# A two-layer decode kernel: VectorE's order inside a head, the place of TensorE's loops in the fetched code, and the order of the work between the layers

## The chip, the core and the metric

The kernel runs on one core of one Trainium2 chip. The metric is device time in microseconds (us) of one execution; less is better. All engines of the core (TensorE, VectorE, ScalarE, GpSimd and SyncE) run their own instruction streams and wait for one another on semaphores. SyncE here does nothing but start DMA transfers.

## What is computed

Two layers over one token for a batch of 2 (width D = 576), each layer an attention over a cache and a mixer MLP, with one set of weights and one cache used in both layers:

```python
def _A_ref(x, k_cache, v_cache, wq, wo):        # H, Dh = 32, 128; Sk = 16384
    q = (x @ wq).reshape(B, Sq, H, Dh).transpose(0, 2, 1, 3)
    scores = einsum("bhqd,bhkd->bhqk", q, k_cache) * (Dh ** -0.5)
    p = softmax(scores, axis=-1)
    o = einsum("bhqk,bhkd->bhqd", p, v_cache)
    return o.transpose(0, 2, 1, 3).reshape(B, Sq, H * Dh) @ wo

def _B_ref(x, w1, w2, w3, w4):
    h = gelu(layernorm(x) @ w1)
    ...                                          # quarters of h shifted along S, which is 1: all zero
    hs = concatenate([g0, g1, g2, g3]) @ w2
    x1 = x + hs
    return x1 + gelu(layernorm(x1) @ w3) @ w4

for layer in range(2):
    x = x + _A_ref(layernorm(x), k_cache, v_cache, wq, wo)
    x = x + _B_ref(layernorm(x), w1, w2, w3, w4)
```

The caches are 2 x 32 x 16384 x 128 in bf16, so each layer reads 268 MB of K and as much of V: 64 pairs of batch and head (called heads from here on), each with one K tile and one V tile of 4.19 MB. Of layer 0's tiles three of K and two of V stay for layer 1.

## The kernel before, in words

**Memory.** One SBUF buffer `mem` holds six places of 32 KB per partition (`slot`, L451) and a small area ahead of them for transposed K (`kt`). A K or V tile fills one place; the parts of the weights wo, w3, w4 and wq share two places between the layers (`plan_all`, L509). The list of transfers is fixed in that function, and `Store.pump` (L291) hands them to SyncE strictly in that order: a transfer is issued (L98) when its place has been released by its last reader, and everything behind it on SyncE waits with it.

**Waits.** Every operation is recorded in a `Graph` with the names that it reads and writes; `_add` (L49) finds what it depends on and `_waits` (L118) leaves out whatever is already covered by another wait of the same engine. An operation can be recorded with `to=`, which means that its semaphore is one that only that engine reads. If another engine has to wait for such an operation, `_stand_in` (L136) takes the next operation of the same engine that raises the general semaphore. When a tile has landed, GpSimd passes it on to TensorE and VectorE as a relay (`landed`, L1099; "POOLq L187" in the profile).

**One head.** Its 128 blocks of 128 keys are split. Half of K goes over TensorE in eight chunks of eight blocks: transposes (L1161), evacuation by ScalarE (L1177), scores with q as a column (L1187). The other half goes over VectorE in four pairs of a product (L1218) and a sum (L1222), with q broadcast over the partitions (`qb`). Then VectorE takes the maximum (L1228, L1230, L1232), GpSimd the maximum over partitions (L1235), ScalarE the exponentials (L1243, L1245, L1249), and TensorE multiplies p with V in four chunks (`pv`, L1275); VectorE keeps the sum (`keep_o`, L1256). The next head's q is prepared by `q_broadcast` (L1115): q as a column (L1112), the diagonal of q (L1118) on VectorE, a matmul with ones (L1122) on TensorE, a copy (L1125) on ScalarE.

**The loops.** `attention` (L1001) records 63 heads in turns of three and has TensorE, ScalarE and VectorE run them as a loop of 21 turns (`Fori`, L253). Three heads make one turn. In head s of the loop the K side of s runs beside the softmax and the V side of head s - 1. `head_slot` says at which instruction of a fetched block of code the loop's first instruction is to stand; it is 0 for all three. In VectorE's order within a head, `keep_o` and the maximum of head s - 1 come behind the second pair, and q of head s + 1 behind the fourth.

**Between the layers.** `last_head` (L1068) finishes layer 0's last head, normalises all heads (`shares`, `normed`), sorts them for the projection (`dealt`; its selection matrix `every` lies in the buffer of the products) and multiplies with wo in five steps (`heads_projection` over `rows_step`, L903). Each step frees its place for the next weights. `two_norms` (L746) computes both layer norms of the mixer at once, `spread_tail` (L794) spreads the last 64 columns of x, `cols_projection` (L830) does w3 and then wq, `between_norms` (L768) keeps the sum for later, `gelu` and `groups_projection` do w4, `input_norm` and `q_projection` give layer 1's q. Idle time of TensorE and ScalarE is used for layer 1's first head, whose K is held: `ahead` (L672) records transposes of it, `lay` (L689) writes them back transposed. When q is there, `early_scores` (L1194) needs only matmuls, 14 chunks of them; VectorE's share of these scores is copied to `s_dve` (L1041), and layer 1's loop begins.

The order of VectorE in a head is set by these lines of `attention`, where c counts the eight chunks and n is 4:

```python
if c % n in (0, 2):
    self.dots(l, s, u, c // n, c % n // 2)
if c == 2 * n - 2:
    self.q_broadcast(s + 1)
if c == LEAD:                       # 2
    self.keep_o(s - 2)
    self.softmax_max(s - 1)
```

Of the kernel before, what the change touches and what calls it, by code (L numbers as in the profile page):

```python
# [5 lines left out]
ALU = mybir.AluOpType  # L6
# [5 lines left out]
LN_EPS = 1e-5  # L12
# [20 lines left out]
class Graph:  # L33
# [111 lines left out]
    def emit(self):  # L145
        nc = self.nc
        self._waits()
        for o in self.all:
# [3 lines left out]
            if o.relay:  # L152
                o.needed = True
        for e, first, n, turns, _ in self.loops:
# [38 lines left out]
        def runner(e):  # L193
            ops = self.ops[e]
            loops = {first: x for en, first, *x in self.loops if en == e}

            def run(eng):
                seen, taken = {}, {}
                i = 0
                while i < len(ops):  # L200
                    if i in loops:
                        n, turns, step = loops[i]
                        self._loop(eng, e, i, n, turns, step, taken, seen, sems, wait, needs, emit_op)
# [13 lines left out]

    def _loop(self, eng, e, first, n, turns, step, taken, seen, sems, wait, needs, emit_op):

# [32 lines left out]
        me = eng.engine  # L252
        with self.nc.Fori(0, (turns - 1) * step + 1, step, engines=OrderedEngineSet([me]), head_slot={me: 0}) as turn:  # L253
            self.shift = turn
# [78 lines left out]
class KB:  # L333
# [13 lines left out]
    WO_CUT = 5  # L347
    PK = ["prod", "gT", "hf", "every"]
    GROUPS = (6, 6, 6, 6, 6, 3, 2, 1)

    def __init__(self, nc, A_x, K, V, wq, wo, w1, w2, w3, w4, out):
# [157 lines left out]
    def plan_all(self):  # L509
# [236 lines left out]
    def two_norms(self, l):  # L746
# [8 lines left out]
        self.tt(s[:, 5, :], self.mv[:, 0, :], hm[:, 0, :], ALU.mult, ["mv", "hm"], ["s5"])  # L755
        self.tt(s[:, 5, :], self.mv[:, 2, :], s[:, 5, :], ALU.subtract, ["mv", "s5"], ["s5"])
        self.stt(s[:, 5, :], s[:, 5, :], 2.0, s[:, 3, :], ALU.mult, ALU.mult, ["s5", "s3"], ["s5"])
        self.tt(s[:, 4, :], s[:, 4, :], s[:, 5, :], ALU.add, ["s4", "s5"], ["s4"])
        self.recip(s[:, 6, :], s[:, 4, :], ["s4"], ["s6"])
# [3 lines left out]
        self.centred(self.x, "x")  # L763
        self.tt(self.kb(self.y0), self.kb(self.xc), self.over_k(s[:, 3, :]), ALU.mult, ["prod", "s3"], ["prod"])
        self.tt(self.kb(self.y), self.kb(self.y0), self.hsc[:, :, :], ALU.add, ["prod", "hsc"], ["prod"])
        self.tt(self.xn[:, :, :], self.kb(self.y), self.over_k(s[:, 7, :]), ALU.mult, ["prod", "s7"], ["xn"])

    def between_norms(self):  # L768

        KT, TL = self.KT, self.TL  # L770
        n, y0 = KT - 1, self.kb(self.y0)
        self.tt(self.x1[:, 0:n, :], y0[:, 0:n, :], self.hs[:, 0:n, :], ALU.add, ["prod", "hs"], ["x1"])
        self.tt(self.x1[TL:, n, :], y0[TL:, n, :], self.hs[TL:, n, :], ALU.add, ["prod", "hs"], ["x1"])
        self.dv(lambda e: e.tensor_copy(out=self.xb[:, 0:n, :], in_=y0[:, 0:n, :]), reads=["prod"], writes=["xb"])
        self.dv(lambda e: e.tensor_copy(out=self.xb[TL:, n, :], in_=y0[TL:, n, :]), reads=["prod"], writes=["xb"])
        self.tt(self.x, self.x, self.x1[:, :, :], ALU.add, ["x", "x1"], ["x"])
# [195 lines left out]
    def groups_projection(self, l):  # L972
        n = len(self.GROUPS)
        for i, (a, b) in enumerate(self.cuts["w4", l]):
            nm = ("w4", l, i)
            self.rows_step(self.store.buf(nm), a, b, self.mps, lambda k: self.gT[:, k * self.B:(k + 1) * self.B],
                           "gT", "mps", nm, i == 0)
            if i < 5:
                self.ahead(l, 1)
            if i < 6:  # L980
                self.lay(l, 1)
# [19 lines left out]
    def attention(self, l):  # L1001
# [27 lines left out]
        else:  # L1029
            self.lay(0, len(self.laid))  # L1030
            assert self.made == len(self.early) and len(self.held_over) == LEAD
            pend += self.held_over
            for h, b, col in sorted(self.early):
                self.early_scores(l, o[0], h * self.BP + b, col)
                if (h, b) == (0, self.CH):
                    self.q_broadcast(1)
            self.store.claim("kt", 0, self.AUX)
            for x in pend:
                self.evacuate(x[3])
            w = self.NB - 2 * self.PB  # L1040
            self.dv(lambda e: e.tensor_copy(out=self.s_dve[0][:, 0:w], in_=self.sps[2][:, 2 * self.PB:self.NB]),  # L1041
                    reads=[("sps", 2)], writes=[("s_dve", 0)], to="vector")
# [25 lines left out]
    def last_head(self, l, s, u):  # L1068
# [4 lines left out]
        i, hg = self.ident[:, :], self.HG  # L1073
        every = bass.AP(tensor=i.tensor, offset=i.offset, ap=[list(i.ap[0]), [1, hg], [0, hg], [hg, 128 // hg]])
        self.dv(lambda e: e.tensor_copy(out=self.every.rearrange("p (j h m) -> p j h m", j=hg, h=hg), in_=every),
                reads=["ident"], writes=["prod", "every"])
        self.softmax_max(s)
        self.keep_o(s - 1)
# [7 lines left out]
        self.landed("v", u, False)  # L1086
        self.pv(l, s, u, 0)
        self.heads_projection(l, 0)
        for g in range(1, 4):
            self.pv(l, s, u, g)  # L1090
        self.keep_o(s, None)
        self.normed(l, first, U)
        self.heads_projection(l, 1)
        self.dealt(late, U, self.sps[0], ("sps", 0), self.masked[1], self.oB[:, :], "oB")
        for i in range(2, len(self.cuts["wo", l])):
# [19 lines left out]
    def q_broadcast(self, s):  # L1115
        i = s % self.NS
        self.q_column(s)
        self.dv(lambda e: e.tensor_scalar(out=self.diag[:, :], in0=self.ident[:, :], scalar1=self.g.column(self.q_f, s),  # L1118
                                          scalar2=None, op0=ALU.mult), reads=["ident", "q_f"], writes=["diag"],
                to="tensor")  # L1120
        qps = self.sps[i][:, 256:384]
        self.pe(lambda pe: pe.matmul(qps, lhsT=self.ones_bf[:, :], rhs=self.diag[:, :],  # L1122
# [71 lines left out]
    def early_scores(self, l, u, b0, col):  # L1194

        to = 0 if col < 2 * self.PB else 2
        ps = self.sps[to]

        nm, buf, keys = self.tile("k", u, b0, self.CH)

        def f(pe):
# [3 lines left out]
            return ins  # L1205
        self.pe(f, reads=[("q_col", 0)] + keys, writes=[("sps", to)])
        self.used(l, "k", u, b0, self.CH)
# [157 lines left out]
```

## Time and profile before

| what | value |
|---|---|
| runs | 2554.43, 2555.88 and 2558.73 us, median 2555.88 |
| the profiled execution | 2555.16 us |
| its span, from the first to the last instruction | 2553.4 us |
| mean granted clock of TensorE | 0.572 |
| busy TensorE, VectorE, ScalarE, GpSimd | 64%, 74%, 48%, 6% of the span |
| moved by DMA | 1094.82 MB in 44761 packets, 429 GB/s over the span |

The profile is one execution as the hardware recorded it. Rows of the timeline give the start in us from the first instruction, the duration (of a group of operations of one kind, up to the last), the engine, the line in the kernel, the operation, what is written and read and in what shape, and how many; a bracket at the end is the idle time of that engine ahead of it and what ended it, where "issue" means that nothing in the profile explains the idle time. Engine names are PE for TensorE, DVE for VectorE, ACT for ScalarE, POOL for GpSimd, SPq for SyncE's queue of DMA starts; "PEld" is the loading of a matmul's weights. Rows of the DMA view give the number of transfers, the size of one and the us from issue to landing. Rows of the table by stage give the stage, its length, the busy time of PE, PEld, DVE, ACT and POOL with the number of instructions in brackets, the granted clock, the share of time in which the DMA engines were busy (it can come out above 1), and GB/s.

### The profile page before, as it was taken

The numbers are of one execution on the slowest core, as the hardware profiler recorded it, in microseconds if no ns is written. First come the engines' busy times: TensorE is split into PE (matmuls) and PEld (weight loads), VectorE is DVE, ScalarE is ACT, GpSimd is POOL, SyncE is SP. The second block draws the span as 40 slices with busy tenths as digits, with TensorE's granted clock in tenths as the row PEclk, the third lists the DMA queues.
The fourth block names the chain that finished last, engine by engine and source line by source line (L and its number), as shares of the span: only waits on it lengthen the run. The fifth ranks groups of instructions, "written<-read, shape, count | busy, mean of one in ns | idle before, by whom it ended". The sixth has DMA issues, their size and how long they took to land.

```text
span 2553.4 us, 75093 instructions
## 1 busy us (share of the span) xinstructions
PE 1629.1 (64%) x34456; PEld 1592.5 (62%) x34456; DVE 1889.3 (74%) x1924; ACT 1215.6 (48%) x1831; POOL 160.5 (6%) x151
## 2 busy tenths in 40 slices
PE   3766666656666665666687756666665666666566
PEld 3766566656656665666677756656665666666565
DVE  4877777777777777777649877777777777777774
ACT  2544444544444454444456544444454444445442
POOL 0000000000000000000000000000000000000000
PEclk8555655555555555555555565555555555555555
DMA  9999999999999999999999999999999999999999
GB/s 410 429 433 431 432 432 431 432 431 433 431 432 432 432 433 430 434 430 432 424 398 428 431 432 432 431 432 431 433 431 433 431 431 433 432 432 431 432 432 383
DMA packets 44761, 1094.82 MB, mean 429 GB/s; under 512 B 4906, under 2 KB 6318, under 8 KB 9390
## 3 DMA queue, kind: packets, MB, share of 16 engines
q1 hardware_dynamic: 44718, 1094.23, 99.9%
q8 instruction: 29, 0.48, 0.1%
q14 instruction: 14, 0.11, 0.0%
HBM read 1094.21 MB, written 0.00 MB: 429 GB/s over the span
## 4 chain that ended last, share of the span: by engine, by line
DMA 63%; DVE 21%; issue 9%; PE 5%; DVEq 0%; SPq 0%; ACT 0%; POOLq 0%; ACTq 0%
DMA mem<-in_A_k_cache_dram 61%; DVE prod L1218 10%; DVE s_dve L1222 9%; DMA mem<-in_B_w_dram 2%; PE tps L1161 2%; PE mps L1275 2%; PE sps L1122 1%; DMA mem<-in_A_wq_dram 0%; PE sps L1187 0%; DVE diag L1118 0%; PE sps L903 0%; DVE mx L1232 0%; DVE q_col L1112 0%; DVE o_acc L1256 0%; DVE mx L1230 0%
## 5 line engine op out<-in xcount | busy, mean ns | idle before, releaser
L1177 ACT ACTIVATE mem<-tps 128x1024 bf16<-128x1024 bf16 x1018 | 1030.1, 1024 | 848.5 <-PE tps L1161 826.8
L1222 DVE TENSOR_REDUCE s_dve<-prod 128x16 f32<-128x2048 bf16 x508 | 1161.2, 2286 | 17.4
L1161 PE MATMUL tps<-ident,mem 128*128 128x128 bf16 x8256 | 1011.0, 301 | 152.9 <-POOLq L187 148.1
L1218 DVE TENSOR_TENSOR prod<-mem,qb 128x2048 bf16<-128x2048 bf16 x508 | 621.3, 1223 | 534.0 <-POOLq L187 512.2
L1275 PE MATMUL mps<-p,mem 128*128 128x1 bf16 x16384 | 515.5, 166 | 605.7 <-ACT p L1249 605.7
L1275 PEld LDWEIGHTS mps<-p,mem 128*128 128x128 bf16 x16384 | 487.8, 105 | 616.5 <-ACT p L1249 616.4
L1161 PEld LDWEIGHTS tps<-ident,mem 128*128 128x128 bf16 x8256 | 770.0, 136 | 162.5 <-POOLq L187 157.4
L1187 PEld LDWEIGHTS sps<-q_col,mem 128*128 128x128 bf16 x8144 | 410.5, 113 | 5.0 <-ACT mem L1177 4.8
L1187 PE MATMUL sps<-q_col,mem 128*128 128x1 bf16 x8144 | 398.2, 170 | 4.3 <-ACT mem L1177 4.1
L1235 POOL PARTITION_ALL_REDUCE mx<-mx x128 | 158.6, 1239 | 2339.4 <-DVE mx L1232 2339.4
L1243 ACT ACTIVATE mx<-mx 128x1 f32<-128x1 f32 x128 | 25.9, 203 | 338.8 <-POOL mx L1235 338.8
L1122 PE MATMUL sps<-diag,ones_bf 128*128 128x128 bf16 x129 | 37.0, 287 | 114.0 <-DVE diag L1118 113.9
L1122 PEld LDWEIGHTS sps<-diag,ones_bf 128*128 128x128 bf16 x129 | 13.4, 104 | 124.6 <-DVE diag L1118 124.6
L1125 ACT ACTIVATE qb<-sps 128x128 bf16<-128x128 f32 x129 | 35.8, 278 | 61.7 <-PE sps L1122 61.7
L1245 ACT ACTIVATE p<-s_dve,mx 128x64 bf16<-128x64 f32 x128 | 44.5, 348 | 15.4
L1249 ACT ACTIVATE p<-sps,mx 128x64 bf16<-128x64 f32 x128 | 37.6, 293 | 0.0
L1230 DVE TENSOR_REDUCE mx<-sps 128x1 f32<-128x64 f32 x128 | 27.3, 213 | 6.2 <-PE sps L1187 6.2
L1118 DVE TENSOR_SCALAR diag<-ident,q_f 128x128 bf16<-128x128 bf16 x129 | 31.6, 245 | 0.0
L1228 DVE TENSOR_REDUCE mx<-s_dve 128x1 f32<-128x64 f32 x128 | 26.6, 208 | 0.0
L830 PE MATMUL sps<-xn,mem 128*128 128x2 bf16 x544 | 21.5, 174 | 6.7 <-DMA mem<-in_A_wq_dram 4.8
L1256 DVE COPY o_acc<-mps 128x1 f32 (+1 forms) x130 | 19.2, 148 | 8.4 <-PE mps L1275 8.4
L830 PEld LDWEIGHTS sps<-xn,mem 128*128 128x128 bf16 x544 | 20.6, 122 | 7.8 <-DMA mem<-in_A_wq_dram 5.5
(113 smaller groups left out, 229.1 us busy)
## 6 DMA issues: line engine op xcount, KB each, us to landing
mem<-in_A_v_cache_dram SPq DMA_DIRECT2D x125, 4096.0 KB, 47.2
mem<-in_A_k_cache_dram SPq DMA_DIRECT2D x124, 4096.0 KB, 40.9
mem<-in_B_w_dram SPq DMA_DIRECT2D x10, 864.0 KB, 15.3
mem<-in_A_wq_dram SPq DMA_DIRECT2D x8, 1024.0 KB, 12.6
mem<-in_B_w_dram SPq DMA_DIRECT2D x7, 1152.0 KB, 15.4
mem<-in_A_wo_dram SPq DMA_DIRECT2D x6, 1152.0 KB, 35.8
mem<-in_A_v_cache_dram SPq DMA_DIRECT2D x4, 1024.0 KB, 8.8
mem<-in_A_k_cache_dram SPq DMA_DIRECT2D x2, 2048.0 KB, 10.2
```

Source lines behind the costliest of these rows:

```text
L830: ins = pe.matmul(out[:, m * B:(m + 1) * B], lhsT=buf[:, c:c + 127 * d + 1:d], rhs=self.xn[:, k, :], start=first and m == lo, stop=False, ...
L1122: self.pe(lambda pe: pe.matmul(qps, lhsT=self.ones_bf[:, :], rhs=self.diag[:, :], start=True, stop=True, skip_group_check=True), reads=["o ...
L1125: self.act(lambda e: e.activation(out=self.qb[s % self.NS][:, :], in_=qps, func=ACT.Copy), reads=[("qps", i)], writes=[("qb", s % self.NS) ...
L1161: ins = pe.transpose(self.tps[t][:, j * 128:(j + 1) * 128], buf[:, j * 128:(j + 1) * 128], self.ident[:, :])
L1177: self.act(lambda e: e.activation(out=self.kt[k], in_=self.tps[t][:, :].rearrange("p (i c) -> p i c", i=self.CH), func=ACT.Copy), reads=[( ...
L1187: ins = pe.matmul(self.sps[sp][:, c * self.CH + j:c * self.CH + j + 1], lhsT=self.kt[k][:, j, :], rhs=self.q_col[:, sp:sp + 1], start=True ...
L1218: self.dv(lambda e: e.tensor_tensor(out=prod, in0=buf.rearrange("p (j d) -> p j d", d=128), in1=qbc, op=ALU.mult), reads=[("qb", s % self. ...
L1222: self.dv(lambda e: e.tensor_reduce(out=sd[:, c0:c0 + DB], in_=prod, axis=AX.X, op=ALU.add), reads=["prod"], writes=[("s_dve", s % self.NS ...
L1235: self.pool(lambda e: e.partition_all_reduce(self.mx[:, 3, m:m + 1], self.mx[:, 2, m:m + 1], channels=128, reduce_op=ROP.max), reads=[("mx ...
L1245: self.act(lambda e: e.activation(out=p[:, n:self.NB], in_=self.s_dve[s % self.NS][:, :], func=ACT.Exp, bias=self.mx[:, 4, m:m + 1], scale ...
L1249: self.act(lambda e: e.activation(out=p[:, 0:n], in_=self.sps[i][:, 0:n], func=ACT.Exp, bias=self.mx[:, 4, m:m + 1], scale=self.scale, acc ...
L1275: ins = pe.matmul(self.mps[:, 448:449], lhsT=buf[:, j * 128:(j + 1) * 128], rhs=p[:, col:col + 1], start=(h == 0 and b == 0), stop=(h == 1 ...
```

## The change

Five edits (the numbers are only for reading):

1. **VectorE in a head.** In a head of the loop `keep_o`, the maximum and the next head's q column and diagonal come directly behind the first pair of products, ahead of the other three. The matmul and the copy that follow the diagonal are recorded ahead of the exponentials (c == 4), not at c == 6.
2. **The loops' places.** TensorE's loop starts at slot 200 of a fetched block in layer 0 and at slot 60 in layer 1; ScalarE's and VectorE's stay at 0.
3. **The last head.** The copy into `every` comes behind the maximum; all four p x V chunks and the sums come ahead of the first projection with wo; `ahead` and `lay` are dealt out anew.
4. **Norms and w3.** In `two_norms` the operations are reordered, and y0 and y get names of their own. The first rows of w3 come in two halves (w3 then has seven transfers instead of six).
5. **Early scores.** They run in the order in which the list has them (VectorE's share first), and VectorE's share goes to `mps` instead of `sps[2]`, so that its copy is recorded after eight of the 14 chunks.

```diff
-    def loop(self, first, turns, step):
+    def loop(self, first, turns, step, slot):
...
-            self.loops.append((e, a, n // turns, turns, step))
+            self.loops.append((e, a, n // turns, turns, step, slot if e == "tensor" else 0))
...
-        with self.nc.Fori(..., head_slot={me: 0}) as turn:
+        with self.nc.Fori(..., head_slot={me: slot}) as turn:
...
+    HEAD = (200, 60)
...
-        self.plan_cols("w3", 0, self.w3, [full(0, mt, a), full(1, mt, a + w3r), full(2, mt, a + 2 * w3r),
-                                          full(4, mt, a + 3 * w3r), (3, 0, mt // 2, 0), (3, mt // 2, mt, a)])
+        self.plan_cols("w3", 0, self.w3, [(0, 0, mt // 2, a), (0, mt // 2, mt, a + w3r // 2),
+                                          full(1, mt, a + w3r), full(2, mt, a + 2 * w3r), full(4, mt, a + 3 * w3r),
+                                          (3, 0, mt // 2, 0), (3, mt // 2, mt, a)])
...
         self.ahead(l, 3)
-        self.scale_of()
+        (s0, s5, s1, s5, s2, centred, s3, s4, s5, y0, s4, y, s6, s7: each operation as before, in this order)
...
-            for h, b, col in sorted(self.early):
+            w = self.NB - 2 * self.PB
+            for i, (h, b, col) in enumerate(self.early):
                 self.early_scores(l, o[0], h * self.BP + b, col)
-                if (h, b) == (0, self.CH):
+                if i == 1:
                     self.q_broadcast(1)
+                if i == w // self.CH - 1:
+                    self.dv(lambda e: e.tensor_copy(out=self.s_dve[0][:, 0:w], in_=self.mps[:, 2 * self.PB:self.NB]),
+                            reads=["mps"], writes=[("s_dve", 0)], to="vector")
...
-            self.dv(lambda e: e.tensor_copy(out=self.s_dve[0][:, 0:w], in_=self.sps[2][:, 2 * self.PB:self.NB]),
-                    reads=[("sps", 2)], writes=[("s_dve", 0)], to="vector")
...
                 step(s, c, True)
-                if c % n in (0, 2):
-                    self.dots(l, s, u, c // n, c % n // 2)
-                if c == 2 * n - 2:
-                    self.q_broadcast(s + 1)
                 if c == LEAD:
                     self.keep_o(s - 2)
                     self.softmax_max(s - 1)
+                    self.q_diag(s + 1)
+                if c % n in (0, 2):
+                    self.dots(l, s, u, c // n, c % n // 2)
                 if c == n:
+                    self.q_spread(s + 1)
                     self.softmax_exp(s - 1)
...
-        self.g.loop(first, (U - 1) // NS, NS)
+        self.g.loop(first, (U - 1) // NS, NS, self.HEAD[l])
...
-        self.dv(lambda e: e.tensor_copy(out=self.every..., in_=every), reads=["ident"], writes=["prod", "every"])
         self.softmax_max(s)
         self.keep_o(s - 1)
+        self.dv(lambda e: e.tensor_copy(out=self.every..., in_=every), reads=["ident"], writes=["prod", "every"])
...
+        self.ahead(l, 2)
         self.softmax_exp(s)
         self.touch(ACT.Sqrt)
-        self.lay(l, 1)
-        self.shares(first, U)
+        self.lay(l, 3)
         self.landed("v", u, False)
-        self.pv(l, s, u, 0)
-        self.heads_projection(l, 0)
-        for g in range(1, 4):
+        for g in range(4):
             self.pv(l, s, u, g)
+        self.shares(first, U)
         self.keep_o(s, None)
+        self.heads_projection(l, 0)
         self.normed(l, first, U)
-        self.heads_projection(l, 1)
         self.dealt(late, U, self.sps[0], ("sps", 0), self.masked[1], self.oB[:, :], "oB")
+        self.heads_projection(l, 1)
+        self.ahead(l, 1)
+        self.lay(l, 1)
...
     def q_broadcast(self, s):
-        (column, diagonal, matmul with ones, copy)
+        self.q_diag(s)      # column, diagonal
+        self.q_spread(s)    # matmul with ones, copy
```

More of the change, by code (lines that the diff above doesn't have):

```diff
@@ L153, in emit @@
                 o.needed = True
-        for e, first, n, turns, _ in self.loops:
+        for e, first, n, turns, *_ in self.loops:
             for i in range(n):
@@ L201, in run @@
                     if i in loops:
-                        n, turns, step = loops[i]
-                        self._loop(eng, e, i, n, turns, step, taken, seen, sems, wait, needs, emit_op)
+                        n, turns, step, slot = loops[i]
+                        self._loop(eng, e, i, n, turns, step, slot, taken, seen, sems, wait, needs, emit_op)
                         i += n * turns
@@ L216, in emit, with _loop @@
                     sect(runner(e))
-    def _loop(self, eng, e, first, n, turns, step, taken, seen, sems, wait, needs, emit_op):
+    def _loop(self, eng, e, first, n, turns, step, slot, taken, seen, sems, wait, needs, emit_op):
         ops = self.ops[e]
@@ L252, in _loop @@
         me = eng.engine
-        with self.nc.Fori(0, (turns - 1) * step + 1, step, engines=OrderedEngineSet([me]), head_slot={me: 0}) as turn:
+        with self.nc.Fori(0, (turns - 1) * step + 1, step, engines=OrderedEngineSet([me]), head_slot={me: slot}) as turn:
             self.shift = turn
@@ L347 @@
     WO_CUT = 5
-    PK = ["prod", "gT", "hf", "every"]
+    PK = ["prod", "gT", "hf", "every", "y0", "y"]
     GROUPS = (6, 6, 6, 6, 6, 3, 2, 1)
+    HEAD = (200, 60)
     def __init__(self, nc, A_x, K, V, wq, wo, w1, w2, w3, w4, out):
@@ L762, in two_norms @@
         self.lay(l, 4)
[L763 to L766, printed above, removed]
+        self.tt(self.xn[:, :, :], y, self.over_k(s[:, 7, :]), ALU.mult, ["y", "s7"], ["xn"])
     def between_norms(self):
@@ L1081, in last_head @@
         self.dealt(0, late, self.sps[2], ("sps", 2), self.masked[0], self.oA[:, :], "oA")
+        self.ahead(l, 2)
         self.softmax_exp(s)
         self.touch(ACT.Sqrt)
-        self.lay(l, 1)
-        self.shares(first, U)
-        self.landed("v", u, False)
-        self.pv(l, s, u, 0)
-        self.heads_projection(l, 0)
-        for g in range(1, 4):
-            self.pv(l, s, u, g)
-        self.keep_o(s, None)
-        self.normed(l, first, U)
-        self.heads_projection(l, 1)
-        self.dealt(late, U, self.sps[0], ("sps", 0), self.masked[1], self.oB[:, :], "oB")
+        self.lay(l, 3)
+        self.landed("v", u, False)
+        for g in range(4):
+            self.pv(l, s, u, g)
+        self.shares(first, U)
+        self.keep_o(s, None)
+        self.heads_projection(l, 0)
+        self.normed(l, first, U)
+        self.dealt(late, U, self.sps[0], ("sps", 0), self.masked[1], self.oB[:, :], "oB")
+        self.heads_projection(l, 1)
+        self.ahead(l, 1)
+        self.lay(l, 1)
         for i in range(2, len(self.cuts["wo", l])):
@@ L1194, in early_scores @@
     def early_scores(self, l, u, b0, col):
-        to = 0 if col < 2 * self.PB else 2
-        ps = self.sps[to]
+        ps, pk = (self.sps[0], ("sps", 0)) if col < 2 * self.PB else (self.mps, "mps")
         nm, buf, keys = self.tile("k", u, b0, self.CH)
@@ L1205, in f @@
             return ins
-        self.pe(f, reads=[("q_col", 0)] + keys, writes=[("sps", to)])
+        self.pe(f, reads=[("q_col", 0)] + keys, writes=[pk])
         self.used(l, "k", u, b0, self.CH)
```

32 lines of the change are left out of this document (20 added, 12 removed).

## The prediction

> **What bounds the kernel now.** I read the page's head, queues and transfers first, then the busy table by stage, then the timeline of one head.
>
> ```profile
> span 2553.4 us, 75093 instructions
> ...
> q8 instruction: 29, 0.48, 0.1%
> ...
> HBM read 1094.21 MB, written 0.00 MB: 429 GB/s over the span
> ...
> mem<-in_A_v_cache_dram SPq DMA_DIRECT2D x125, 4096.0 KB, 47.2
> mem<-in_A_k_cache_dram SPq DMA_DIRECT2D x124, 4096.0 KB, 40.9
> ```
>
> The kernel is a stream of 1094 MB, and a K needs 40.9 us to land: it stands in a queue. The table by stage says where the stream is not at its rate:
>
> ```profile
> 100.00:1260.00 1160.00, 731.76 (x15375) 716.93 (x15373) 877.48 (x841) 557.83 (x839) 75.19 (x60) 0.57 1.00 432
> 1260.00:1282.00 22.00, 17.72 (x431) 16.95 (x429) 6.97 (x36) 6.28 (x14) 0.35 (x1) 0.50 0.98 395
> 1282.00:1294.00 12.00, 9.78 (x217) 9.20 (x216) 0.98 (x6) 5.28 (x8) 0.00 (x0) 0.50 0.97 354
> 1294.00:1330.00 36.00, 27.66 (x592) 26.16 (x589) 14.85 (x34) 18.62 (x26) 1.25 (x1) 0.50 1.02 427
> 1330.00:1352.00 22.00, 18.36 (x405) 18.05 (x403) 20.31 (x20) 12.54 (x18) 1.25 (x1) 0.58 0.96 395
> 1352.00:2510.00 1158.00, 744.38 (x15677) 729.62 (x15675) 892.96 (x855) 568.06 (x855) 76.42 (x61) 0.57 1.00 431
> ```
>
> The last number of a row is GB/s. Both long stages run at 431 to 432. Only the seam between the layers loses: 22 x (1 - 395/432) = 1.9, 12 x (1 - 354/432) = 2.2, 36 x (1 - 427/432) = 0.4 and 22 x (1 - 395/432) = 1.9 us, together 6.4 us. That is all that this change could win there, and whatever it adds to those gaps it pays in full, because from 1352 on the stream never pauses again: the end shifts as the stream shifts. 0.2% of the run, 5.1 us, is about what a measurement of this kernel can tell from no change.
>
> **The change part by part.** First the heads in the long stages, where VectorE's order is new:
>
> ```profile
> 716.76 0.33 SPq L98 DMA_DIRECT2D mem<-in_A_k_cache_dram  x1
> ...
> 720.17 0.33 SPq L98 DMA_DIRECT2D mem<-in_A_v_cache_dram  x1
> ...
> 719.03 1.23 DVE L1218 TENSOR_TENSOR prod<-mem,qb 128x2048 bf16<-128x2048 bf16 x1 [4.54 <-POOLq L187]
> ...
> 726.52 0.16 DVE L1232 TENSOR_TENSOR mx<-mx 128x1 f32<-128x1 f32 x1
> ...
> 729.17 1.01 PE L1275 MATMUL mps<-p,mem 128*128 128x1 bf16 x32 [4.92 <-ACT p L1249]
> ...
> 733.99 0.29 PE L1122 MATMUL sps<-diag,ones_bf 128*128 128x128 bf16 x1 [0.82 <-DVE diag L1118]
> ...
> 736.21 0.33 SPq L98 DMA_DIRECT2D mem<-in_A_k_cache_dram  x1
> ```
>
> K landed at about 718.9 and frees VectorE. The maximum moves ahead of one pair of product and sum, so it comes some 3.6 us earlier (726.5 to 722.9), and the 0.82 us for which TensorE waited on the diagonal goes. What is late next is V: issued 3.4 us after its K and landing after 47.2 instead of 40.9 us, it arrives 9.7 us behind K, at 728.6, against the 729.17 at which p x V starts now. So TensorE gains about 0.5 + 0.8 us per head, all of it in front of a wait for the next K. Worth: **0**.
>
> The same move adds a wait that the diff doesn't name. Today SyncE's K transfer waits on TensorE alone: TensorE waits for the diagonal, which stood behind VectorE's last sums, so that wait covered VectorE's reading of the tile. With the diagonal in front of three of the four pairs it no longer does, and in the changed program's list of waits every K transfer of the loops names VectorE too. The helper takes VectorE's next operation that raises the general semaphore: the next head's maximum (L1232). A tile's successor is therefore issued only 4.1 us into the next head: 742.9 instead of 736.21, with its V queued behind it on SP. In the long stages that is free: a K needs 40.9 us to land of which its own 4.19 MB at 432 GB/s are 9.7, so 31 us of work stand ahead of it and 24 would still. Price there, **0**; cover gone, it would be 6.7 us once per pause.
>
> The weights' stage. TensorE's first projection with wo comes after all 128 p x V columns instead of after 32:
>
> ```profile
> 1264.06 0.80 SPq L98 DMA_DIRECT2D mem<-in_A_wo_dram  x2
> ...
> mem<-in_A_wo_dram SPq DMA_DIRECT2D x1, 432.0 KB, 9.9
> ...
> 1267.76 1.21 PE L903 MATMUL sps<-oA,mem 128*128 128x2 bf16 x40
> 1268.83 2.70 PE L1275 MATMUL mps<-p,mem 128*128 128x1 bf16 x96
> ...
> 1269.00 14.05 SPq L98 DMA_DIRECT2D mem<-in_B_w_dram  x6
> ...
> 1281.14 1.57 PE sps L830 x36
> ...
> 1282.73 4.94 DMA mem<-in_B_w_dram
> ```
>
> That projection frees the place of w3's first rows, issued at 1269.00. It moves behind 2.7 us of p x V, 1.0 of sums and two transposed chunks (1.8), against about 1.5 us by which the last scores, rid of the diagonal, come earlier and 1.1 of a reordered copy: issue near 1271.9, 2.9 later. The last wo landed at 1264.5 + 9.9 = 1274.4. What does a transfer into an empty queue cost? The last row: 576 KB issued at 1282.73 land 4.94 later, 1.37 of it at 432 GB/s, so 3.6 us ahead of the data. w3 then starts at 1275.5: **+1.1** us. In return its first rows come in two parts: 18 of the 36 matmuls (0.8 us) free the place of the sixth part, issued at about 1281.9 instead of 1282.73, when w3's other parts, now 1.1 later, still fill the queue. That gap (4.94 less 1.37 less what the queue still held, 2.9, so 0.7) goes, and of the next ones, 2.2 us in the row 1282 to 1294 all told, about half. The shorter chain of the norm (0.4 us, the centred x and one product off it) stays behind 24 transposes on TensorE (2.7 us). Sum **0**, with -2 (all of 1282 to 1294 won) and +1.5 (only the late w3) as its ends.
>
> The entry into layer 1's loop:
>
> ```profile
> 50.10 1.23 DVE L1218 TENSOR_TENSOR prod<-mem,qb 128x2048 bf16<-128x2048 bf16 x1 [4.08 <-issue]
> ...
> 1314.00 0.16 DVE L858 CAST q_col<-sps 128x1 bf16<-128x1 f32 x1 [8.38 <-PE sps L830]
> ...
> 1314.97 2.74 PE L1203 MATMUL sps<-q_col,mem 128*128 128x1 bf16 x96
> ...
> 1317.75 0.23 DVE L1041 COPY s_dve<-sps 128x64 f32<-128x64 f32 x1 [2.92 <-PE sps L1203]
> ...
> 1318.52 1.22 DVE L1218 TENSOR_TENSOR prod<-mem,qb 128x2048 bf16<-128x2048 bf16 x1 [0.55 <-issue]
> ...
> 1321.67 1.03 PE L1161 MATMUL tps<-ident,mem 128*128 128x128 bf16 x8 [3.96 <-issue]
> ```
>
> TensorE stood 3.96 us for nothing that the profile shows; since the queues list instruction packets (q8), I read such waits as code being fetched. With the loop's head in the block that it is already in, I take 0. But VectorE is ahead of it there: it waited for the last of 96 early scores, and now copies after the first 64 of 112 (48 of the 96: 1.4 us instead of 2.74), so its first pair starts at 1318.52 - 1.3 = **1317.2**. Layer 0's loop gains nothing: TensorE had no such stall there, VectorE had one (4.08) that stays.
>
> What follows is the sum:
>
> ```profile
> 1334.11 1.22 DVE L1218 TENSOR_TENSOR prod<-mem,qb 128x2048 bf16<-128x2048 bf16 x1 [0.69 <-ACT qb L1125]
> ...
> 1337.69 1.22 DVE L1218 TENSOR_TENSOR prod<-mem,qb 128x2048 bf16<-128x2048 bf16 x1
> ...
> 1341.59 0.16 DVE L1232 TENSOR_TENSOR mx<-mx 128x1 f32<-128x1 f32 x1
> ...
> 1317.74 8.85 SPq L98 DMA_DIRECT2D mem<-in_A_k_cache_dram  x2
> ...
> mem<-in_A_k_cache_dram SPq DMA_DIRECT2D x1, 4096.0 KB, 15.3
> ...
> 1326.26 9.76 SPq L98 DMA_DIRECT2D mem<-in_A_k_cache_dram  x2
> ...
> mem<-in_A_k_cache_dram SPq DMA_DIRECT2D x1, 2048.0 KB, 8.7
> ...
> 1353.20 0.33 SPq L98 DMA_DIRECT2D mem<-in_A_v_cache_dram  x1
> ...
> mem<-in_A_v_cache_dram SPq DMA_DIRECT2D x1, 4096.0 KB, 21.6
> ```
>
> Here the queue is nearly empty. K of head 0 lands at 1317.74 + 15.3 = 1333.0. Behind it come the two halves of head 1's K, into the place of the loop's first head: now issued at 1326.26 (that head's own maximum covers the first two pairs) and 1335.7. In the changed program both wait for the maximum of the head after. VectorE's head is 1334.11 - 0.69 - 1318.52 = 14.9 us, the maximum ends 1341.75 - 1337.69 = 4.1 us into the next one: both issued at 1317.2 + 14.9 + 4.1 + 0.1 = 1336.3, ten microseconds late for the first half, with the queue empty since 1333.0. The second half now shows the restart: issued at 1335.7, landed 8.7 later, 4.9 of it data, so 3.8. From 1336.3 on: 3.8, then 16.8 MB (two halves, V, K, V) at 9.7 per 4.19 MB, 38.8: that V lands at 1378.9. It lands at 1353.20 + 21.6 = 1374.8 now. After it the queue stays full in both. **+4.1 us**: 7.1 us of empty queue (1333.0 to 1340.1) in place of today's gaps there.
>
> [...]
>
> Sum: 0 + 0 + 0 + 4.1. The profiled execution took 2555.16 us (span 2553.4), so 2559.3; the median of the runs, 2555.88, lies 0.7 above it: **2560.0**.
>
> **Rivals.** (a) *VectorE's entry stalls* (slower). Its loop still starts at slot 0 of a block. At 1318.52 that cost 0.55 us, at 50.10 it cost 4.08. In the changed program VectorE has one instruction less ahead of the loop and arrives 1.3 us sooner; if the block is not asked for before the loop, a whole stall like the 4.08 and 3.96 of the rows follows the copy's end (1317.98 - 1.3 = 1316.7) and puts the first pair at 1320.7, 3.5 later than I take; if it is asked for shortly before, half of that, 1.7. The hole grows by the same, so the sum is +5.8 to +7.6, in the middle +6.7: 2562.6. It decides as soon as the pair starts after 1318.2. For it: VectorE's own stall at layer 0. Against: 0.55 in the same place now. [...]
>
> (b) *The queue doesn't run dry* (no difference, or a little faster). If the weights' stage wins its 2 us and the halves' wait turns out to be covered by what is queued (V in four parts, K), today's 1.9 us of 1330 to 1352 go too: -2 to +1.5, 2555.6. Against it: 19 us between VectorE's entry and the issue are VectorE's own work.
>
> (c) *The slots aren't what they say*: if the code ahead ends beyond slot 60, TensorE stands its 4 us as now. VectorE's maximum then waits for TensorE's scores by some 0.7 us: 2560.7, within the forecast. More than 5.1 us faster would need nearly the whole 6.4.
>
> **How the numbers follow.** Forecast 0.58, of which 0.12 lies beyond +5.1; (a) 0.24, nearly all beyond it (0.22); (b) 0.14; the rest, 0.04, faster through what I don't see. Slower by over 0.2%: 0.34; faster: 0.04; same: 0.62. Range: the weights' stage from -2 and the restart at the 1.9 us shorter end give +0.2 and with half of (b) 2555.4; (a) with the late w3 (+1.5) gives +8.2, 2564.1.
>
> **What would show it.** In the profile after: both halves of that K issued within half a microsecond of each other near 1336, straight behind VectorE's second maximum of layer 1; a hole of some 7 us in the DMA share around 1337; 432 GB/s from 1345 on; K issues in the long stages 4 us after a K landed and no change of their period; w3's first issue near 1272; TensorE's 3.96 gone. Wrong would be: a period of heads that moves (fetches on the back edge), VectorE's first pair before 1316 or after 1318.5, or a seam whose gaps shrink.

## The result, and the profile after

The changed kernel takes 2560.47 us (median of 21 runs, 2559.70 to 2561.82), the kernel before 2556.08 us in as many runs (2554.43 to 2558.73). The ratio is 1.0017 with a 95% interval of 1.0010 to 1.0023: **4.4 us slower**, where 4.1 were forecast.

The table by stage, in the same stages as before:

```profile
100.00:1260.00 1160.00, 720.82 (x15385) 708.38 (x15382) 880.22 (x840) 543.72 (x839) 23.51 (x60) 0.57 1.00 432
1260.00:1282.00 22.00, 18.99 (x426) 18.40 (x424) 7.50 (x38) 8.71 (x17) 1.17 (x1) 0.50 0.95 377
1282.00:1294.00 12.00, 10.16 (x218) 9.40 (x216) 0.81 (x5) 5.00 (x8) 0.00 (x0) 0.50 1.01 408
1294.00:1330.00 36.00, 26.43 (x591) 24.11 (x590) 15.42 (x36) 15.91 (x25) 0.39 (x1) 0.55 1.02 415
1330.00:1352.00 22.00, 19.25 (x415) 18.97 (x412) 21.42 (x21) 13.55 (x19) 0.39 (x1) 0.58 0.70 285
1352.00:2510.00 1158.00, 727.14 (x15546) 714.54 (x15543) 891.35 (x849) 549.88 (x850) 23.90 (x61) 0.57 1.00 432
```

Both long stages stand at 432 GB/s (432 and 431 before). The three stages up to 1330 lose 2.8 + 0.7 + 1.4 = 4.9 us of stream against 4.5 before (each the stage's length times the share missing to 432). The stage from 1330 to 1352 loses 22 x (1 - 285/432) = 7.5 us against 1.9. So nearly all of the price is made here: +5.6 in this stage, +0.4 ahead of it. (The two profiled executions lie 6.7 us apart, the medians 4.4.)

What stands in that stage, from VectorE's, SyncE's and the DMA engines' rows (the last two rows are the DMA view from 1331.7 to 1338.5, in 40 slices):

```profile
1317.15 0.23 DVE L1045 COPY s_dve<-mps 128x64 f32<-128x64 f32 x1 [1.64 <-PE mps L1217]
1317.95 1.23 DVE L1232 TENSOR_TENSOR prod<-mem,qb 128x2048 bf16<-128x2048 bf16 x1 [0.58 <-issue]
...
1330.62 2.29 DVE L1236 TENSOR_REDUCE s_dve<-prod 128x16 f32<-128x2048 bf16 x1
1333.04 1.23 DVE L1232 TENSOR_TENSOR prod<-mem,qb 128x2048 bf16<-128x2048 bf16 x1
...
1336.94 0.16 DVE L1246 TENSOR_TENSOR mx<-mx 128x1 f32<-128x1 f32 x1
...
1337.18 0.80 SPq L98 DMA_DIRECT2D mem<-in_A_k_cache_dram  x2
...
GB/s 0 0 0 0 0 0 0 0 0 0 0 0 0 0 0 0 0 96 0 0 0 0 0 0 0 0 0 0 0 0 0 0 0 0 0 0 0 96 771 482
DMA packets 22, 0.25 MB, mean 36 GB/s; under 512 B 7, under 2 KB 7, under 8 KB 7
```

VectorE has read the last of the tile at 1332.9 (1330.62 + 2.29). The two transfers go out at 1337.18, directly behind the next head's maximum (1336.94 + 0.16), and from 1331.7 to 1338.5 the queue moves 0.25 MB, where 6.8 us hold 2.9 MB at 432 GB/s. From there on nothing is made up, as the V that the sum was made to shows (issued at 1352.64, 1353.20 before):

```profile
1352.64 0.97 SPq L98 DMA_DIRECT2D mem<-in_A_v_cache_dram  x1
...
mem<-in_A_v_cache_dram SPq DMA_DIRECT2D x1, 4096.0 KB, 27.3
```

It lands at 1379.9, 5.1 us later than before (1374.8). This profiled execution, 2561.82 us, is the slowest of the 21. It lies another 1.6 us further from before's than those 5.1; 0.5 of them lie outside the spans (2559.6 and 2553.4 us), the rest comes behind this V, and neither is explained here.

How the stream starts again shows in the first half's landing and in the first 1.8 us of its data:

```profile
mem<-in_A_k_cache_dram SPq DMA_DIRECT2D x1, 2048.0 KB, 7.2
...
1338.20:1340.00 1.80, 1.28 (x29) 1.14 (x27) 1.77 (x2) 1.77 (x3) 0.00 (x0) 0.94 0.88 255
```

The first half lands 7.2 us after its issue, 2.3 more than its data take at 432 GB/s, and the queue is still below its rate, at 255 GB/s, until 1340.

The heads of the long stages, at the place shown of before:

```profile
723.03 0.16 DVE L1246 TENSOR_TENSOR mx<-mx 128x1 f32<-128x1 f32 x1
...
728.82 0.99 PE L1289 MATMUL mps<-p,mem 128*128 128x1 bf16 x32 [4.33 <-POOLq L187]
...
742.70 0.33 SPq L98 DMA_DIRECT2D mem<-in_A_k_cache_dram  x1
```

The maximum is there 3.5 us earlier, and p x V starts 0.35 us earlier and no more: it now waits for V's landing (POOLq) in place of ScalarE's exponentials. K's successor goes out at 742.70 in place of 736.21, and the rate does not fall.

TensorE at the entry into layer 1's loop has lost its 3.96 us; no idle time is noted at its first transposes:

```profile
1318.25 1.01 PE L1176 MATMUL tps<-ident,mem 128*128 128x128 bf16 x8
```

### The profile page after: what moved, and what is told of

Its sections match the earlier page's. It is cut to its first block, busy times and chain, and to the rows that moved or that the text cites. A ratio compares the mean times of both kernels' runs of the same rounds, so it can differ in the third digit from the quotient of the medians.

```text
span 2559.6 us, 75212 instructions
## 1 busy us (share of the span) xinstructions
PE 1608.3 (63%) x34456; PEld 1575.1 (62%) x34456; DVE 1894.9 (74%) x1924; ACT 1186.5 (46%) x1831; POOL 53.6 (2%) x151
## 4 chain that ended last, share of the span: by engine, by line
DMA 83%; DVE 7%; PE 5%; issue 4%; SPq 1%; POOLq 0%; DVEq 0%; ACT 0%
DMA mem<-in_A_k_cache_dram 77%; PE tps L1176 4%; DVE prod L1232 3%; DMA mem<-in_B_w_dram 2%; DVE s_dve L1236 2%; DMA mem<-in_A_v_cache_dram 2%; DMA mem<-in_A_wo_dram 2%; PE sps L1202 1%; SPq L98 0%; DMA mem<-in_A_wq_dram 0%; PE mps L1289 0%; DVE mx L1246 0%; DVE o_acc L1270 0%; DVE mx L1244 0%; DVE mx L1242 0%
## 5 line engine op out<-in xcount | busy, mean ns | idle before, releaser
L1289 PE MATMUL mps<-p,mem 128*128 128x1 bf16 x16384 | 507.1, 165 | 546.2 <-POOLq L187 527.0
L1289 PEld LDWEIGHTS mps<-p,mem 128*128 128x128 bf16 x16384 | 476.9, 104 | 562.4 <-issue 542.0
L1249 POOL PARTITION_ALL_REDUCE mx<-mx x128 | 51.7, 404 | 2449.4 <-DVE mx L1246 2449.4
L1137 PE MATMUL sps<-diag,ones_bf 128*128 128x128 bf16 x129 | 30.2, 234 | 10.3 <-DVE diag L1130 10.2
L1263 ACT ACTIVATION_READ_ACCUMULATOR p<-sps,mx (+1 forms) x128 | 24.2, 189 | 0.0
L1259 ACT ACTIVATION_READ_ACCUMULATOR p<-s_dve,mx (+1 forms) x128 | 23.8, 186 | 0.0
```

Source lines behind the costliest of these rows:

```text
L1249: self.pool(lambda e: e.partition_all_reduce(self.mx[:, 3, m:m + 1], self.mx[:, 2, m:m + 1], channels=128, reduce_op=ROP.max), reads=[("mx ...
L1259: self.act(lambda e: e.activation(out=p[:, n:self.NB], in_=self.s_dve[s % self.NS][:, :], func=ACT.Exp, bias=self.mx[:, 4, m:m + 1], scale ...
L1263: self.act(lambda e: e.activation(out=p[:, 0:n], in_=self.sps[i][:, 0:n], func=ACT.Exp, bias=self.mx[:, 4, m:m + 1], scale=self.scale, acc ...
L1289: ins = pe.matmul(self.mps[:, 448:449], lhsT=buf[:, j * 128:(j + 1) * 128], rhs=p[:, col:col + 1], start=(h == 0 and b == 0), stop=(h == 1 ...
```

## The experiments

The theory on trial: **the whole difference is the moment at which the two halves of the second K of layer 1's loop are issued**, and that moment is set by which VectorE operation stands in for "this tile has been read". The rivals: the weights' stage (later projection, halved w3), the loops' new places, the order in the heads itself, or a seam in which an earlier K would only move the hole. Each kernel was timed in turns with the kernel before on its chip; differences are between medians of the same chip.

**1. Release K behind its own last pair.** A tiny copy (0.14 us) that raises the general semaphore becomes the stand-in.

```diff
+    def dots_done(self, s, i):
+        k = i * self.NS + s % self.NS
+        self.dv(lambda e: e.tensor_copy(out=self.done[:, k:k + 1], in_=self.eps[:, :]), reads=["eps"], writes=[("done", k)])
...
                     self.dots(l, s, u, c // n, c % n // 2)
+                if c == 2 * n - 2:
+                    self.dots_done(s, 1)
```

> The changed kernel with one more tiny copy on VectorE behind the fourth pair of each head; it raises the general semaphore and so becomes what K's transfers wait for, in place of the next head's maximum. Theory (the wait costs it all): VectorE's fourth pair of layer 1's first head in the loop ended at 1332.91, so both halves of that K are issued at 1333.1 instead of 1337.18 and the time falls by 4.1 us from the changed kernel's 2560.5: 2556.4 (2555.6 to 2557.2). Rival (in this seam the stream goes by when places come free, an earlier K only moves the hole behind it): no more than 1 us gained, 2559.5 to 2560.7. Rival (the later first projection or the new place of the loops costs it): 2560.5.

Measured: 2556.65 us, +0.6 to before (ratio 1.0000, 0.9991 to 1.0009). Both halves went out at 1332.11, behind the pair's end:

```profile
1332.11 0.80 SPq L98 DMA_DIRECT2D mem<-in_A_k_cache_dram  x2
```

One copy of 0.14 us takes back nearly all of the loss; both rivals fall.

**2. The same behind the second pair as well.**

```diff
-                if c == 2 * n - 2:
-                    self.dots_done(s, 1)
+                if c in (n - 2, 2 * n - 2):
+                    self.dots_done(s, c // n)
```

> As the kernel with one copy behind the fourth pair, and the same behind the second, so that K's first half waits for two pairs alone. Theory (the wait): first half issued at 1326.1, second at 1333.1, with the data of the K before ending at 1331.7 and that of the first half at 1336.6, so no hole is left: the V of the loop's head lands about 7 us ahead of the changed kernel's 1379.9, at 1372.5 to 1373.5, and the time is 2553.5 (2552.5 to 2554.5), below the kernel before. Rival (places come free too late): not below 2556. Rival (another part of the change): 2560.5.

Measured: **2553.10 us** (2552.44 to 2554.33), -2.9 to before, ratio 0.9989 (0.9980 to 0.9998): faster than the changed kernel by 7.3 us and than the kernel before by 0.1%, at the edge of what these runs can tell. The rows, with the stage and the V (the DMA row is that of the V issued at 1349.16):

```profile
1324.23 0.33 SPq L98 DMA_DIRECT2D mem<-in_A_k_cache_dram  x1
...
1331.47 0.33 SPq L98 DMA_DIRECT2D mem<-in_A_k_cache_dram  x1
...
1330.00:1352.00 22.00, 18.43 (x384) 18.15 (x382) 21.57 (x27) 13.52 (x19) 0.78 (x2) 0.59 1.01 427
...
1349.16 0.33 SPq L98 DMA_DIRECT2D mem<-in_A_v_cache_dram  x1
...
mem<-in_A_v_cache_dram SPq DMA_DIRECT2D x1, 4096.0 KB, 22.9
```

427 GB/s in place of 285: the hole is gone, and that of before (395) with it. The copies cost the stream nothing in the long stages (432 GB/s in both). The halves went out 1.6 to 1.9 us earlier than expected, because VectorE entered the loop at 1316.31 in this execution and not at 1317.95.

**3. The old order in a head, all else changed.**

```diff
                 step(s, c, True)
-                if c == LEAD:
-                    self.keep_o(s - 2)
-                    self.softmax_max(s - 1)
-                    self.q_diag(s + 1)
                 if c % n in (0, 2):
                     self.dots(l, s, u, c // n, c % n // 2)
+                if c == 2 * n - 2:
+                    self.q_broadcast(s + 1)
+                if c == LEAD:
+                    self.keep_o(s - 2)
+                    self.softmax_max(s - 1)
                 if c == n:
-                    self.q_spread(s + 1)
                     self.softmax_exp(s - 1)
```

> The changed kernel with the order of VectorE in a head as it was before (the maximum behind the second pair, q behind the fourth), all its other edits kept. Theory (the wait): first half of K issued at 1326.26 - 0.57 = 1325.7, second at 1335.1, as VectorE enters the loop 0.57 us earlier than before; the weights' stage is worth +0.1; so 2555.5 (2554.8 to 2556.5). Rival (the other edits cost it): 2559 to 2560.5.

Measured: 2556.37 us, +0.3 (0.9991 to 1.0009). The other four edits together are worth nothing that can be measured.

**4. The new order alone on the kernel before.** The reverse of 3.

> The kernel before with the new order of VectorE in a head alone. Theory (the wait): VectorE enters layer 1's loop at 1318.52, the maximum of the head after ends 19.1 us on, both halves of K are issued at 1337.8 and the V behind lands 42.7 later, at 1380.5, 5.6 us later than before: 2561.7 (2560.9 to 2562.5), more than the whole change. Rival (the other edits cost it): 2556.0. Both in part: between 2557 and 2560.

Measured: 2561.71 us, +5.7 (1.0012 to 1.0030), issue at 1338.85. The new order alone does more harm than the whole change. The expected number was met in part by luck: VectorE entered the loop 0.7 us earlier than expected (1317.80), and its first maximum then stood 1.74 us for TensorE's scores, which the expectation does not have:

```profile
1323.28 0.22 DVE L1236 TENSOR_REDUCE mx<-sps 128x1 f32<-128x64 f32 x1 [1.74 <-PE sps L1193]
```

No kernel here moved the maximum without the diagonal or the reverse. That it is the diagonal's move which adds the wait is read from the programs: with the diagonal behind the fourth pair, before and in kernel 3, no tile's transfer has to wait for VectorE.

**5. The block behind the second pair.**

```diff
-                if c == LEAD:
-                    ...
                 if c % n in (0, 2):
                     self.dots(l, s, u, c // n, c % n // 2)
+                if c == LEAD:
+                    self.keep_o(s - 2)
+                    self.softmax_max(s - 1)
+                    self.q_diag(s + 1)
```

> The changed kernel with the whole block (sum kept, maximum, q column, diagonal) behind the second pair instead of the first. Theory (the wait): the first half of K goes behind its own head's maximum, issued at 1326.3, and its data end at 1336.6; the second half waits for the next head's maximum, now 3.6 us later, issued at 1340.6, with data from 1342.3 on. The hole is 5.7 us against 6.8 in the changed kernel, and the next K follows 0.3 late: 2559.4 (2558.5 to 2560.2). If a hole behind half a K cost nothing: 2556. If the wait of the first half alone counted: 2556 too.

Measured: 2559.73 us, +3.1 (1.0004 to 1.0022). First half at 1323.97, second at 1339.06: a late second half alone still costs most of it (3.1 of 4.4), as the theory has it.

**6. TensorE's loops at slot 0.**

```diff
-    HEAD = (200, 60)
+    HEAD = (0, 0)
```

> The changed kernel with TensorE's two loops at slot 0 of a block as before. By the prediction TensorE stands some 4 us again at layer 1's entry, VectorE's first maximum there waits about 0.7 us for its scores and the halves of K with it: 2561.2 (2560.4 to 2562.0). If the loop's place in the code cost TensorE time on each turn (21 turns a layer): several us either way. If VectorE's second maximum does not notice: 2560.5.

Measured: 2564.21 us, +7.6 (1.0018 to 1.0039), 3.2 above the changed kernel's +4.4. The prediction's price for this, 0.7, was wrong:

```profile
1322.82 1.04 PE L1176 MATMUL tps<-ident,mem 128*128 128x128 bf16 x8 [3.70 <-issue]
...
1325.15 0.23 DVE L1244 TENSOR_REDUCE mx<-sps 128x1 f32<-128x64 f32 x1 [2.73 <-PE sps L1202]
...
1340.73 0.80 SPq L98 DMA_DIRECT2D mem<-in_A_k_cache_dram  x2
```

TensorE stands 3.70 us at the entry of layer 1's loop. VectorE's first maximum, now behind one pair instead of two, waits 2.73 us for TensorE's scores, and the K halves wait for VectorE. In the long stages nothing moves (432 GB/s in both), so it is an entry's price and not one per turn. The edit moves layer 0's loop as well, but at that entry nothing changes: TensorE waits there for ScalarE, 3.95 us here and 3.94 in the changed kernel. Of the 3.5 us by which the halves go out later than in the changed kernel, 0.7 are a later entry of VectorE in this execution (1318.69 against 1317.95). With the early maximum TensorE's old place costs more, +7.6 and +5.7 (kernel 4) against +4.4; with the late maximum the new place costs nothing that can be measured (+0.3, kernel 3).

**7. The first projection back, on top of 2.**

```diff
-        for g in range(4):
-            self.pv(l, s, u, g)
-        self.shares(first, U)
-        self.keep_o(s, None)
-        self.heads_projection(l, 0)
+        self.pv(l, s, u, 0)
+        self.heads_projection(l, 0)
+        for g in range(1, 4):
+            self.pv(l, s, u, g)
+        self.shares(first, U)
+        self.keep_o(s, None)
```

> The kernel with the copies behind the second and the fourth pair (2553.1) and the first projection with wo back behind the first p x V chunk. Theory (the later projection costs what the gap ahead of w3 shows, 0.9 us: two slices of 1 us at 264 and 211 GB/s): w3's first rows issued near 1268 instead of 1270.9, no gap behind wo, and 2552.2 (2551.6 to 2553.0). Rival (the chain of o, wo and the norms is what comes late in this stage, so an earlier w3 only waits in the queue, and the sums come later): 2553.1 or up to 1 us more.

Measured: 2553.68 us, -2.9 (0.9979 to 0.9997), the same as 2. The first parts of w3 go out at 1267.91 instead of 1270.89, and nothing is won: the stage 1260 to 1282 stays (390 GB/s, 389 in kernel 2), and the stage 1282 to 1294 falls from 418 to 390. The rival's number holds; that the chain of o, wo and the norms is what comes late there fits, but is not shown by itself.

```profile
1282.00:1294.00 12.00, 10.33 (x214) 9.75 (x212) 0.81 (x5) 5.54 (x7) 0.00 (x0) 0.50 1.00 390
```

**8. w3's first rows whole.**

```diff
-        self.plan_cols("w3", 0, self.w3, [(0, 0, mt // 2, a), (0, mt // 2, mt, a + w3r // 2),
+        self.plan_cols("w3", 0, self.w3, [full(0, mt, a),
```

> The changed kernel with w3's first rows in one transfer again. The stage from 1282 to 1294 went from 354 to 408 GB/s with the change, which is 1.5 us; if that is the halves' doing, it is lost again: 2561.5 to 2562.0. If it is that all of w3 comes later and keeps the queue filled, nothing is lost: 2560.5.

Measured: 2560.91 us, +4.3 (1.0008 to 1.0026), the changed kernel's +4.4. The stage stays at 413 GB/s (408): the halves are worth nothing.

**9. Slot 0 on top of 2.** If a stall at the entry costs only by way of the K halves, enough slack there should swallow it.

> The kernel with the copies behind the second and the fourth pair (2553.1), TensorE's loops at slot 0 as in the run where that cost the changed kernel some 3.5 us. Theory (a stall at the loop's entry costs only by way of the K halves, and only from the point where they miss the end of the queue): VectorE's maximum again waits 2.7 us for TensorE's scores, the second half of K is issued at 1331.5 + 3.5 = 1335.0, before the data of the first half end at 1336.2, so the queue hardly runs dry: 2553.1 to 2554.2. Rival (the stall of TensorE or VectorE is itself on the path): 2556.0 to 2556.8.

Measured: 2556.64 us, -0.3 (0.9989 to 1.0007), 2.7 above kernel 2: **a miss**, inside the rival's range. The second half was issued when the expectation said:

```profile
1335.07 0.33 SPq L98 DMA_DIRECT2D mem<-in_A_k_cache_dram  x1
...
mem<-in_A_k_cache_dram SPq DMA_DIRECT2D x1, 2048.0 KB, 8.7
...
1327.91 0.33 SPq L98 DMA_DIRECT2D mem<-in_A_k_cache_dram  x1
...
mem<-in_A_k_cache_dram SPq DMA_DIRECT2D x1, 2048.0 KB, 9.8
```

The first half landed at 1327.91 + 9.8 = 1337.7 and the second 8.7 us after its issue, at 1343.8: 6.1 us behind the first, where 4.9 are its data. So 1.2 us of gap although the issue came 2.6 us ahead of the landing. In kernel 2 it came 6.4 us ahead, and the second half landed 4.7 us behind the first, without a gap. The next K of kernel 9, issued at 1350.15, 3.4 us ahead of the landing of the V before it (1336.55 + 17.0 = 1353.55), landed 14.7 us after its issue, 11.3 behind that V, where 9.7 are its data: 1.6 us more. With both gaps this V lands 2.5 us later than in kernel 2. So the expectation, which measured the slack to the end of the data, set it too short. This rests on one execution, and that one is the fastest of its eleven: at 2554.72 us it lies only 1.0 above kernel 2's profiled one (2553.74), so the 2.5 us do not all stand in its own time. The time alone does not exclude the rival.

All kernels on one scale: the issue of the halves, the landing of the V behind them (its issue plus its DMA row), and the time.

| kernel | first half | second half | V landed | time to before, same chip |
|---|---|---|---|---|
| 2, copies behind both | 1324.23 | 1331.47 | 1372.1 | -2.9 |
| 7, and projection back | 1324.85 | 1332.01 | 1372.6 | -2.9 |
| 9, and slot 0 | 1327.91 | 1335.07 | 1374.5 | -0.3 |
| before | 1326.26 | 1335.69 | 1374.8 | 0 |
| 1, copy behind the last | 1332.11 | with it | 1375.0 | +0.6 |
| 3, old order | 1324.78 | 1334.21 | 1376.4 | +0.3 |
| 5, block behind the second | 1323.97 | 1339.06 | 1378.5 | +3.1 |
| 8, w3 whole | 1336.85 | with it | 1379.8 | +4.3 |
| changed | 1337.18 | with it | 1379.9 | +4.4 |
| 4, order alone | 1338.85 | with it | 1381.7 | +5.7 |
| 6, slot 0 | 1340.73 | with it | 1383.5 | +7.6 |

Over a spread of 11 us the time follows the V's landing to about 1.3 us (the profiles are single executions, the times medians). The moments of issue can be compared to about 1 us: leaving out the kernel before and kernel 4, whose work ahead of the loop is the old one, VectorE's first pair starts between 1316.25 and 1318.69.

Kernel 3 does not fit the theory on trial as it is worded. Its halves go out 1.5 us earlier than before, and the V lands 1.6 later. Its second half followed the first with a gap of 0.9 us, and the next K, issued at 1349.91 and 3.0 us ahead of the landing of the V before it (1336.13 + 16.8 = 1352.9), landed 16.8 us later at 1366.7, 4.1 more than its data ask. Why that K lost so much is not shown. So the halves' moment explains the loss of the change and its cure, but not every difference of 2 us in this table.

Where the queue had not run empty, a half or the next K that was issued 5 us or more ahead of the landing of the transfer before it left at most 0.3 us of gap (kernels 1, 2 and 7), and one issued 2.3 to 4.5 us ahead left 0.6 to 4.1 us (before, 3, 5, 7 and 9).

## Why the prediction was right

- **The bound** held: both long stages stand at 431 to 432 GB/s before and after, and what is explained of the difference was made between 1260 and 1352.
- **The heads**, forecast 0: maximum at 722.9 forecast, 723.0 to 723.2 measured; the K issue at 742.9 forecast, 742.70 measured; V became what is late next. No loss of rate.
- **The K halves**, forecast +4.1: issue at 1336.3 forecast, 1337.18 measured; the V at 1378.9 forecast, 1379.9 measured. The 0.9 us comes from VectorE's entry (1317.95 against 1317.2), and most of that from q, ready at 1314.67 instead of 1314.00; it is no more than single executions differ in (q was ready at 1313.60 in that of kernel 9 and at 1315.41 in that of kernel 6). From the issue to that V the forecast had 42.6 us (3.8 of restart and four tiles), and 1337.18 to 1379.9 is 42.7; kernels 1, 4 and 6 give 42.9, 42.9 and 42.8.
- **The restart of 3.8 us** was right as a total, and that was partly luck. The prediction means a transfer into an empty queue, but neither of its two rows is one. Before, the first half of that K landed at 1326.26 + 11.7 = 1338.0 (its row stands below), so it was still on its way when the second half went out at 1335.69: the 3.8 are 2.3 of waiting behind the first half and 1.6 of gap. For the row at 1282.73 the prediction itself has 2.9 us of work still in the queue. The changed kernel shows an empty queue: no data to speak of from 1331.7 to 1338.2, a first half that lands 2.3 us above its data, and 255 GB/s until 1340. The stream up to the V is 3.9 us later than its data, so the sum came out; how these 3.9 are made up is not what the prediction describes. The first part of w3, issued at 1271.53, landed 3.9 us later, 2.5 above its data, and not 3.6. The lower end of the range takes the restart 1.9 us shorter, which no run shows: from an issue into the empty queue to that V the runs have 3.9 to 4.1 us above the data (42.7 to 42.9 less 38.8).
- **The weights' stage**, forecast 0: right as a sum (+0.4 in the table by stage, nothing in kernel 3), but not in its terms. It was a late w3 (+1.1) against the halved rows and the gaps (about as much back); kernels 7 and 8 put the price of either at nothing. What both terms missed is that a gap taken away in front comes back further on, as kernel 7 shows; that TensorE's chain through wo and w3 sets when places come free there is a reading of it and not shown.
- **Rival (a)**, VectorE's stall at its entry, did not come: 0.58 us, as before 0.55. **Rival (b)** fails by the hole shown; kernel 2 shows the seam without it, at -2.9. **Rival (c)** did not come either, but its price of 0.7 us, for which the prediction gives no working, was too small by some 2: behind one pair instead of two, the maximum of kernel 6 stood 2.73 us. That the waits at the loops' entries are code being fetched is the prediction's reading and not shown. What the runs show is that TensorE's at layer 1 comes with slot 0 (3.96 us before, 3.98 in kernel 4, 3.70 in kernel 6) and is not noted with slot 60.

The row of before for the first half, issued at 1326.26:

```profile
mem<-in_A_k_cache_dram SPq DMA_DIRECT2D x1, 2048.0 KB, 11.7
```

## What to carry to other kernels

When an operation is moved ahead, list the waits that it used to cover: here TensorE's wait for the diagonal had silently covered "VectorE has read the tile", and moving the diagonal turned that into a wait for an operation of the next head. In the long stages, where a K took 40.9 us to land before, that wait was free for tile after tile (an issue 6.5 us later, 742.70 instead of 736.21, at 432 GB/s still). It was paid at the one place where the queue was nearly empty (the V behind it 5.1 us later). Look for such a place, and issue ahead of the landing before (here 5 us were enough in a queue that had not run empty, and 4.5 left a gap). A semaphore raised by a copy of 0.14 us at the right place, or at two, was worth 3.8 and 7.3 us.

## What the runs showed of the hardware that was not expected

GpSimd's maximum over partitions came down to a third of its time without being touched. In the kernel before its row stands beside a product of VectorE, which begins before it:

```profile
726.60 1.22 DVE L1218 TENSOR_TENSOR prod<-mem,qb 128x2048 bf16<-128x2048 bf16 x1
...
726.77 1.25 POOL L1235 PARTITION_ALL_REDUCE mx<-mx  x1 [18.19 <-DVE mx L1232]
```

In the changed kernel the two small q operations stand between the maximum and the product, and GpSimd is first:

```profile
723.28 0.39 POOL L1249 PARTITION_ALL_REDUCE mx<-mx  x1 [19.04 <-DVE mx L1246]
...
723.38 1.22 DVE L1232 TENSOR_TENSOR prod<-mem,qb 128x2048 bf16<-128x2048 bf16 x1
```

1.25 us against 0.39, with an end 0.2 us behind the product's in the first case. It goes with the order in the other kernels too: 1.25 us on average in kernel 3 (old order), 0.39 in kernels 4 and 5, where the q operations stand between. Why is not shown. The product takes 1.22 us in both rows, also where it begins 0.10 us behind GpSimd's maximum and inside it. The 0.9 us per head were worth nothing, since p was not what the stream waited for: p x V at 728.82 waits for V's landing, and the long stages stand at 432 GB/s.
